# Softmax sums of two pairs of heads in one product of four 32-column blocks, one reciprocal for both, and copies across partitions inside SBUF

## The chip, the cores and the metric

One core of one Trainium2 chip. The metric is the device time of one execution, in microseconds (us). Most numbers below come from the profile of one execution of each kernel, taken on the chip; times of several executions are given as a median with the lowest and the highest.

## The reference, cut to what matters

```python
# 8 batches, 12 heads, 448 rows, 64 columns per head; fp32
q_n, k_n = rmsnorm(q, g_q), rmsnorm(k, g_k)
attn = exp(scores - max);  attn = attn / (sum(attn) + 1e-09)     # scores = q_n k_n^T / 8
x = (attn @ v), heads side by side                               # 3584 x 768
out = silu(x @ w_in) @ w_out                                     # 768 -> 2048 -> 768
```

The kernel works through 48 "pairs" of heads (8 batches x 6). It keeps everything transposed: for one pair, `xT` is 128 partitions (two heads of 64) x 448. The softmax sum of a row is therefore a sum over partitions, made by TensorE as a product with ones, and it arrives in PSUM already repeated over the 64 partitions of its head. In the first batch there are no block products of `x @ w_in` yet to fill TensorE; instead VectorE, ScalarE and GpSimd round the weights. From the second batch on, the block products ("fill") are run between the parts of the attention.

## The kernel before

The parts that the change and the argument touch. One "turn" n of the main loop, cut:

```python
for n in range(last + 2):
    scores(n, 0)                      # L400 products, L405 exponentials -> e[0], e[1]
    weigh(n - 1, 1)                   # L416
    add_up(n - 1, 2, 3); unload(n - 1)
    transpose(n + 1, "q")             # L381
    fill()                            # block products, L508 / L549 (none in the first batch)
    divide(n - 1)                     # sums L445, reciprocal L449, multiplication L451
    scores(n, 1)
    weigh(n, 0); transpose(n + 1, "k"); add_up(n, 1)      # first batch: the k transposes first
    fill()
    weights_in(n, 3); normalise(n + 3)                    # ... cut
```

```python
def add_up(n, *chunks):
    if n < z.NPAIR and 3 in chunks:       # first batch: a second partial sum
        nc.vector.tensor_tensor(out=es_two, in0=e[2], in1=e[3], op=ALU.add)
        return
    for j in chunks:
        nc.vector.tensor_tensor(out=es, in0=e[0] if j == 1 else es, in1=e[j], op=ALU.add)

def unload(n):
    nc.scalar.copy(xU, state[n]["av"])

def divide(n):
    t = ps.tile([P, S], F32, name="tr") if n >= z.NPAIR else bank(S)
    sums = [es, es_two] if n < z.NPAIR else [es]
    for i, part in enumerate(sums):
        for h in range(2):
            nc.tensor.matmul(t[ds(h * D, D), :], ones[0:R, :], part[:, h, :],
                             start=i == 0, stop=i == len(sums) - 1)
    nc.vector.reciprocal(out=r, in_=t)
    engine = nc.gpsimd if n < z.NPAIR else nc.vector
    engine.tensor_tensor(out=xT(*pairs[n]), in0=xU, in1=r, op=ALU.mult)
```

## Time and profile before

| | before |
|---|---|
| median of 4 executions | 1478.93 us (1477.04 to 1480.41) |
| span of the profiled execution | 1474.5 us |
| TensorE / VectorE / ScalarE / GpSimd busy | 1449.3 / 739.8 / 566.2 / 393.4 us |
| sum blocks (TensorE) and reciprocals (VectorE) | 48 and 48 |
| attention | up to about 850 us; then block products alone |

I read three marks, all starts of score products (L400, sixteen instructions a pair): the first of pair 1, the first of pair 7, and the second half of pair 47. "Stretch 1-7" holds turns 1 to 6; "stretch 7-47" the steady attention; what follows is the tail.

### The profile page before, as it was taken

What the parts mean: (1) busy time and instruction counts of PE and PEld (TensorE: products, weight loads), DVE (VectorE), ACT (ScalarE), POOL (GpSimd) and SP (SyncE); (2) the same over time, 40 slices, a digit from 0 to 9 for tenths busy, and PEclk for the clock granted to TensorE, in tenths of its full rate; (3) what the DMA queues carried; (4) which work ended last, traced back from release to release, by engine and by line L of the source; (5) the groups of instructions that cost most, each with busy time, mean ns of one, the idle gap of its engine ahead of it and who ended that gap; (6) DMA issues with size and microseconds to landing.
All of it is one profiled execution on the core that took longest, in us unless ns stands there. A gap on an engine that the chain in (4) does not pass through costs nothing.

```text
span 1474.5 us, 14016 instructions
## 1 busy us (share of the span) xinstructions
PE 1449.3 (98%) x5072; PEld 703.8 (48%) x5072; DVE 739.8 (50%) x928; ACT 566.2 (38%) x931; POOL 393.4 (27%) x250
## 2 busy tenths in 40 slices
PE   5999999999999999999999999999999999999998
PEld 2334444444444444444444445555555555555554
DVE  4887867676755555755554687732222222222220
ACT  5789876555555455545545444400000000000000
POOL 5864532333233333332331044410000000000000
PEclk9999999999999999999999999999999999999999
DMA  6433421221222122211211147522222222222220
GB/s 209 118 100 114 144 83 57 69 63 57 75 82 63 56 63 88 63 57 65 85 50 51 69 152 231 160 82 83 83 80 79 79 79 79 81 84 84 86 68 25
DMA packets 119188, 128.95 MB, mean 87 GB/s; under 512 B 48836, under 2 KB 101316, under 8 KB 119108
## 3 DMA queue, kind: packets, MB, share of 16 engines
q1 hardware_dynamic: 118788, 127.95, 28.2%
q8 instruction: 42, 0.69, 0.2%
q14 instruction: 38, 0.31, 0.1%
q10 hardware_dynamic: 320, 0.00, 0.0%
HBM read 87.56 MB, written 40.37 MB: 87 GB/s over the span
## 4 chain that ended last, share of the span: by engine, by line
PE 92%; DVE 5%; issue 1%; DMA 1%; ACT 0%; POOL 0%; ACTq 0%; SPq 0%; DVEq 0%; POOLq 0%
PE mm L508 35%; PE sc L508 13%; PE sc L400 9%; PE av L416 9%; PE av L508 7%; PE tr L508 7%; PE mm L549 5%; PE tr L445 3%; PE tr L386 1%; PE tr L381 1%; DVE work L449 1%; DVE rms L298 1%; DVE work L433 0%; DVE W L109 0%; DMA W<-in_moe_w_in_dram 0%
## 5 line engine op out<-in xcount | busy, mean ns | idle before, releaser
L405 ACT ACTIVATE work<-sc,rms 112x448 f32<-112x448 f32 x384 | 212.1, 636 | 183.3 <-PE sc L400 148.1
L304 POOL TENSOR_TENSOR rms<-rms,minus_half 112x16 f32<-112x16 f32 (+1 forms) x49 | 175.8, 3588 | 290.9 <-DVE rms L300 271.6
L508 PE MATMUL mm<-x,W 128*128 128x448 f32 x552 | 220.9, 541 | 0.7 <-ACT parts L515 0.6
L528 POOL TENSOR_TENSOR parts<-parts 128x448 f32<-128x448 f32 (+1 forms) x42 | 45.8, 1090 | 630.7 <-DVE parts L459 630.7
L449 DVE RECIPROCAL work<-tr 128x448 f32<-128x448 f32 x42 | 124.2, 2957 | 104.5 <-PE tr L445 104.3
L400 PE MATMUL sc<-work 64*112 64x448 f32 x768 | 170.7, 563 | 1.0 <-ACT work L382 0.6
L508 PE MATMUL mm<-sums_x,W 128*128 128x448 f32 x408 | 165.9, 542 | 0.7 <-DVE stage L459 0.4
L416 PE MATMUL av<-work,rows 112*64 112x448 f32 x768 | 165.5, 552 | 0.0
L433 DVE TENSOR_TENSOR work<-work 112x896 f32<-112x896 f32 x132 | 148.0, 1121 | 1.6
L508 PEld LDWEIGHTS mm<-x,W 128*128 128x128 f32 x552 | 101.9, 190 | 93.0 <-issue 87.9
L400 PEld LDWEIGHTS sc<-work 64*112 64x112 f32 x768 | 61.3, 173 | 103.8 <-issue 82.8
L508 PEld LDWEIGHTS mm<-sums_x,W 128*128 128x128 f32 x408 | 74.9, 190 | 68.9 <-issue 61.4
L459 DVE TENSOR_TENSOR stage<-mm,parts 128x448 f32<-128x448 f32 (+1 forms) x75 | 46.0, 614 | 118.0 <-PE mm L508 66.6
L416 PEld LDWEIGHTS av<-work,rows 112*64 112x64 f32 x768 | 46.6, 136 | 105.3 <-issue 103.8
L459 DVE TENSOR_TENSOR parts<-mm,parts 128x448 f32<-128x448 f32 (+1 forms) x50 | 30.5, 611 | 95.6 <-PE mm L508 95.2
L549 PE MATMUL mm<-x,W 128*128 128x448 f32 x192 | 75.9, 541 | 0.0
L508 PE MATMUL mm<-W,work 128*128 128x384 f32 x204 | 68.6, 486 | 0.0
L515 ACT COPY parts<-mm 128x448 f32<-128x448 f32 (+1 forms) x27 | 14.1, 523 | 141.7 <-PE mm L508 141.7
L508 PE MATMUL sc<-W,work 128*128 128x384 f32 x192 | 64.5, 486 | 0.0
L634 ACT ACTIVATE stage<-stage 128x896 f32<-128x896 f32 x56 | 50.7, 944 | 31.7 <-DVE stage L459 26.0
L405 ACT ACT_TABLE_LOAD x36 | 46.2, 1283 | 34.9 <-issue 23.8
L298 DVE TENSOR_REDUCE rms<-qn 112x8 f32<-112x512 f32 x49 | 33.3, 680 | 44.8 <-ACT qn L297 44.7
(146 smaller groups left out, 1865.0 us busy)
## 6 DMA issues: line engine op xcount, KB each, us to landing
hidden<-stage SPq DMA_DIRECT2D x56, 448.0 KB, 3.0
work<-hidden SPq DMA_DIRECT2D x7, 2048.0 KB, 9.2
x<-hidden SPq DMA_DIRECT2D x7, 2048.0 KB, 8.7
W<-in_moe_w_in_dram SPq DMA_DIRECT2D x24, 512.0 KB, 4.0
rows<-in_moe_w_out_dram SPq DMA_DIRECT2D x32, 384.0 KB, 3.6
rows<-in_q_dram SPq DMA_DIRECT2D x48, 224.0 KB, 3.5
rows<-in_k_dram SPq DMA_DIRECT2D x48, 224.0 KB, 3.3
rows<-in_v_dram SPq DMA_DIRECT2D x48, 224.0 KB, 2.5
```

The costliest lines, as they stand in the source:

```text
L298: nc.vector.tensor_reduce(out=rms[:, i], in_=t, axis=AX.X, op=ALU.add)
L304: nc.gpsimd.tensor_tensor(out=flat, in0=flat, in1=half, op=ALU.pow)
L400: nc.tensor.matmul(banks[:, h, 0:S], kT[rows, ts(j, R)], qT[n % 2][rows, :], start=True, stop=True,)
L405: nc.scalar.activation(e[j][:, h, :], banks[:, h, 0:S], AF.Exp, scale=rms[n % 4][:, 1, h, j : j + 1])
L416: nc.tensor.matmul(st["av"][ds(h * D, D), :], st["v"][:, h, j, :], e[j][:, h, :], start=(j == 0), stop=(j == J - 1),)
L433: nc.vector.tensor_tensor(out=es, in0=e[0] if j == 1 else es, in1=e[j], op=ALU.add)
L449: nc.vector.reciprocal(out=r, in_=t)
L459: nc.vector.tensor_tensor(out=out, in0=a, in1=b, op=ALU.add)
L508: nc.tensor.matmul(t, self.left(name, s), self.right(name, s), start=s == ends[0], stop=s == ends[1])
L528: nc.gpsimd.tensor_tensor(out=u2, in0=u2, in1=p5, op=ALU.add)
L549: nc.tensor.matmul(h, room.w1(c, f), xT(b, c), start=(c == 0), stop=(c == z.NW - 1))
L634: nc.scalar.activation(t, t, AF.Silu)
```

## The change

The intent: a sum needs only 32 of the 64 columns that it was given, so one block of four products (two pairs x two heads, 32 columns each) can serve two pairs, with one reciprocal of 128 partitions for both. Each reciprocal row then exists on 32 partitions and has to be copied to 64, which six small transfers inside SBUF do. Pairs whose result is needed at once (4 and 5 of the first and of the odd batches) stay single. Room for a second `es` and `r` comes from dropping `xU` (the division is now in place in `xT`) and two of the four temporaries of the block products. The first batch loses its second partial sum.

```diff
-    es_two = stage[0:R, 0 : 2 * S].rearrange("p (h s) -> p h s", h=2)
     def add_up(n, *chunks):
-        if n < z.NPAIR and 3 in chunks:
-            nc.vector.tensor_tensor(out=es_two, in0=e[2], in1=e[3], op=ALU.add)
-            return
+        t = es[n % 2]
         for j in chunks:
-            nc.vector.tensor_tensor(out=es, in0=e[0] if j == 1 else es, in1=e[j], op=ALU.add)
+            nc.vector.tensor_tensor(out=t, in0=e[0] if j == 1 else t, in1=e[j], op=ALU.add)
     def unload(n):
-        nc.scalar.copy(xU, state[n]["av"])
+        nc.scalar.copy(xT(*pairs[n]), state[n]["av"])
-    def divide(n): ...                                   # as shown above
+    def is_single(n):
+        b, hp = pairs[n]
+        return hp >= z.NPAIR - 2 and (b == 0 or b % 2 == 1)
+    def sums(members, width):
+        t = ps.tile([P, S], F32, name="tr") if members[0] >= z.NPAIR else bank(S)
+        for h in range(2):
+            for i, n in enumerate(members):
+                nc.tensor.matmul(t[ds(h * D + i * width, width), :], ones[0:R, 0:width],
+                                 es[n % 2][:, h, :], start=True, stop=True)
+        nc.vector.reciprocal(out=r[0], in_=t)
+    def divide(n, t):                                    # in place; GpSimd in the first batch
+        ...
+    def divide_by_sums(n):
+        if n > 2 and n % 2 == 1 and not is_single(n - 2):
+            for i in range(2):
+                divide(n - 3 + i, r[i])
+        if n > 0 and is_single(n - 1):
+            sums([n - 1], D)
+            divide(n - 1, r[0])
+        elif n > 0 and n % 2 == 0:
+            sums([n - 2, n - 1], D // 2)
+            own = [t.rearrange("(h i p) s -> i h p s", h=2, i=2) for t in r]
+            for i in range(2):
+                for h in range(2):
+                    nc.sync.dma_start(own[1][i, h], own[0][1, h])
+            for h in range(2):
+                nc.sync.dma_start(own[0][1, h], own[0][0, h])
     # class Seven (block products):
-            self.p1, self.u2, self.u3, self.p5 = (parts[:, ds(i * S, n)] for i in range(4))
+            self.u2, self.u3 = (parts[:, ds(i * S, n)] for i in range(2))
+            self.p1, self.p5 = done[1, 2], done[2, 1]
     # main loop:
-        if n > 0:
-            divide(n - 1)
+        divide_by_sums(n)
     # ... (allocation sizes, and an argument p1 that goes away, cut)
```

More of the change, by code (lines that the diff above doesn't have):

```diff
@@ L351, in bounded @@
     stage = mem.tile([P, 3 * 2 * S], F32, name="stage")
-    parts = mem.tile([P, 4 * S], F32, name="parts")
-    work = mem.tile([P, 15 * S + 2 * J * D], F32, name="work")
-    qT0, qT1, kT, e0, e1, e2, e3, es, xU, r = divided(
-        work, S, S, S, 2 * S, 2 * S, 2 * S, 2 * S, 2 * S, S, S
+    parts = mem.tile([P, 2 * S], F32, name="parts")
+    work = mem.tile([P, 17 * S + 2 * J * D], F32, name="work")
+    qT0, qT1, kT, e0, e1, e2, e3, es0, es1, r0, r1 = divided(
+        work, S, S, S, 2 * S, 2 * S, 2 * S, 2 * S, 2 * S, 2 * S, S, S
     )
-    qT = [qT0, qT1]
+    qT, r = [qT0, qT1], [r0, r1]
     normal, rms = normal
-    squares = work[0:R, ds(15 * S, 2 * J * D)].rearrange("p (h j d) -> p h j d", h=2, j=J)
+    squares = work[0:R, ds(17 * S, 2 * J * D)].rearrange("p (h j d) -> p h j d", h=2, j=J)
     e = [t[0:R].rearrange("p (h s) -> p h s", h=2) for t in (e0, e1, e2, e3)]
-    es = es[0:R].rearrange("p (h s) -> p h s", h=2)
+    es = [t[0:R].rearrange("p (h s) -> p h s", h=2) for t in (es0, es1)]
     def xT(b, c):
@@ L438, in divide @@
-    def divide(n):
-        t = ps.tile([P, S], F32, name="tr") if n >= z.NPAIR else bank(S)
-        sums = [es, es_two] if n < z.NPAIR else [es]
-        for i, part in enumerate(sums):
-            for h in range(2):
-                nc.tensor.matmul(
-                    t[ds(h * D, D), :], ones[0:R, :], part[:, h, :],
-                    start=i == 0, stop=i == len(sums) - 1,
-                )
-        nc.vector.reciprocal(out=r, in_=t)
-        engine = nc.gpsimd if n < z.NPAIR else nc.vector
-        engine.tensor_tensor(out=xT(*pairs[n]), in0=xU, in1=r, op=ALU.mult)
-        state[n] = None
+        nc.scalar.copy(xT(*pairs[n]), state[n]["av"])
@@ new lines, in is_single @@
+    def is_single(n):
[5 more added lines that the diff above has]
+            for i, n in enumerate(members):
+                nc.tensor.matmul(
+                    t[ds(h * D + i * width, width), :], ones[0:R, 0:width], es[n % 2][:, h, :],
+                    start=True, stop=True,
+                )
+        nc.vector.reciprocal(out=r[0], in_=t)
@@ new lines, in divide @@
+    def divide(n, t):
+        engine = nc.gpsimd if n < z.NPAIR else nc.vector
+        x = xT(*pairs[n])
+        engine.tensor_tensor(out=x, in0=x, in1=t, op=ALU.mult)
+        state[n] = None
+    def divide_by_sums(n):
[11 more added lines that the diff above has]
+                    nc.sync.dma_start(own[1][i, h], own[0][1, h])
+            for h in range(2):
+                nc.sync.dma_start(own[0][1, h], own[0][0, h])
@@ L492, in bounded, with __init__ @@
     class Seven:
-        def __init__(self, left, right, steps, n, done, p1=None):
+        def __init__(self, left, right, steps, n, done):
             self.left, self.right, self.steps, self.n, self.done = left, right, list(steps), n, done
             self.banks = {}
-            self.p1, self.u2, self.u3, self.p5 = (parts[:, ds(i * S, n)] for i in range(4))
-            if p1 is not None:
-                self.p1 = p1
+            self.u2, self.u3 = (parts[:, ds(i * S, n)] for i in range(2))
+            self.p1, self.p5 = done[1, 2], done[2, 1]
         def product(self, name, steps=None):
@@ L579, in sum_x, with part_in @@
         right_sums(*quarters(group, c), *sums_of_x(c))
-    def part_in(group, m, rows, p1=None):
+    def part_in(group, m, rows):
         chunk = 2 * m // room.CHUNK
@@ L601, in part_in @@
         done = {(i + 1, j + 1): rows[i][:, ts(j, S)] for i in range(2) for j in range(2)}
-        return Seven(lambda name, c: lefts[name](c), right, range(HW), S, done, p1)
+        return Seven(lambda name, c: lefts[name](c), right, range(HW), S, done)
     def halves_in(group, blocks, beside=lambda m: iter(()), begun=()):
@@ L752, in start @@
             rows = [staged() for _ in range(2)]
-            begun.append((rows, part_in(group, m, rows, rows[0][:, S:] if m else None)))
+            begun.append((rows, part_in(group, m, rows)))
         return begun
```

## The prediction

> **What bounds the kernel now.** I read the page's busy table and its 40 slices first, then the table of stretches, then the chain of waits in order of time, once in the attention stage with the pipeline full and once in the first batch.
>
> ```profile
> PE 1449.3 (98%) x5072; PEld 703.8 (48%) x5072; DVE 739.8 (50%) x928; ACT 566.2 (38%) x931; POOL 393.4 (27%) x250
> ...
> PE   5999999999999999999999999999999999999998
> PEld 2334444444444444444444445555555555555554
> DVE  4887867676755555755554687732222222222220
> ACT  5789876555555455545545444400000000000000
> ```
>
> TensorE looks full all the way, and VectorE and ScalarE look nearly full too, but only in the first two or three slices (37 us each). A busy TensorE proves little by itself, so the chain has to say whether its instructions really follow one another. With batches 1 to 7 running (90 to 840 us), the chain lies on TensorE almost without a break. This piece is one pair of heads and a bit; the columns are start, length, engine, line, count:
>
> ```profile
> 509.42 5.28 PE mm L508 x14
> 514.70 0.90 PE tr L445 x4
> 515.60 1.69 PE sc L400 x8
> 517.29 1.65 PE av L416 x8
> 518.95 0.53 PE tr L386 x4
> 519.48 2.27 PE mm L508 x6
> 521.75 0.04 issue
> 521.79 3.27 PE mm L508 x8
> 525.07 1.69 PE sc L400 x8
> ```
>
> L445 is the softmax sum: two products of ones with the added exponentials, one per head, in the two 64-column halves of the array. An fp32 product shows as two instructions, so x4. The block takes 0.90 us on the path. The reader should compare 514.70, where the fill products are followed by sums and then scores, with 525.07, where the scores follow the fill products directly: the scores take 1.69 us either way. So dropping a block frees its whole 0.90 us and no switching time stays behind. One pair takes 19.5 us (sums at 514.70, next at 534.22).
>
> In the first batch the chain is another:
>
> ```profile
> 35.13 0.95 DVE work L433
> 36.07 0.34 DVE W L106
> 36.41 0.02 issue
> 36.44 1.26 DVE W L109
> ...
> 39.80 1.00 DVE stage L430
> 40.81 0.04 issue
> 40.85 1.00 PE mm L445 x4
> ...
> 41.94 2.96 DVE work L449
> 44.90 0.95 DVE work L433
> ```
>
> There VectorE sets the pace: one pair every 9.77 us (35.13 to 44.90), made of adding exponentials, waiting 1.00 us for the second half of the sums, a reciprocal of 2.96 us, another add, and rounding weights. This lasts for about five pairs. After 850 us there is no attention left and the change touches only where two temporaries of the block products live.
>
> **What the skill says.** (1) "TensorE: Matmul & The Clock Gate", Part 3: products with few output columns can occupy different column groups at the same time; three 32-column tiles are given as 2.38x measured. The trace agrees for two halves: four instructions in 0.90 us, where four of the full array take 4 x 5.28/14 = 1.51 us. No trace of this kernel has four column groups; this is the main thing to find out. (2) "TensorEngine Tiling (Array Packing)", Key Properties: changing the tiling mode drains the array. The trace shows the size: 0.90 less two slots of 0.377 leaves 0.15 us. (3) "DMA: Bandwidth & Descriptors", Anatomy of one DMA: a transfer has a fixed part of about 2.0 us, mostly the receipt for the last byte, and a semaphore is waited for by the issuing sequencer, not by the DMA engines. The trace agrees in size (the table of DMA issues: KB each, then us to landing):
>
> ```profile
> rows<-in_v_dram SPq DMA_DIRECT2D x48, 224.0 KB, 2.5
> hidden<-stage SPq DMA_DIRECT2D x16, 224.0 KB, 2.0
> ```
>
> So the new copies cost latency, and they hold up the queue that issues them. (4) "Perfetto Trace Analysis", first note: matmul busy time is a bad measure of nearness to the limit. Here the chain gives a reason to trust it anyway, since instruction starts are spaced evenly.
>
> **The change, part by part.** The built program of the changed kernel, listed engine by engine, has 29 sum blocks where there were 48 (six of those double, because the first batch summed two partial tensors): 19 blocks of four 32-column products and 10 blocks of two 64-column products, the latter for pairs 4 and 5 of the first and the odd batches, whose result is needed at once.
>
> *Sum blocks on TensorE.* Outside the first batch 42 blocks become 25 (17 of four products, 8 of two). A four-product block is eight instructions; if four column groups run together that is again two slots of 0.377 plus 0.15 = 0.90 us. Removed: 17 x 0.90 = 15.3 us, all on the path by the comparison above. The weight loads of eight instructions instead of four might add something; I allow 0.1 us a block, 17 x 0.1 = 1.7 us.
>
> *Reciprocals.* 48 become 29: 19 x 2.957 = 56 us less on VectorE. Outside the first batch this is beside the path: the k transposes at L386 follow the weighting 1.65 us after its start, as do the q transposes at L381, which wait for no reciprocal. The tr bank is free in time today (in the timeline one reciprocal ends at 518.61 and the transposes start at 518.95), so nothing is gained.
>
> *First batch.* VectorE loses the reciprocal in pairs without sums and gains one add of about 0.95 us in every pair (the two partial sums were added by TensorE before). A turn without sums: 9.77 - 2.96 - 1.00 - about 0.1 of hand-over + 0.95 = 6.7 us on VectorE. A turn with sums: 9.77 + 0.95 = 10.7 us. Of the turns n = 1 to 5, sums fall in 2, 4 and 5. VectorE's own need is 3 x 10.7 + 2 x 6.7 = 45.5 us against 48.9 now, a gain of 3.4 us if the turns can lend time to each other. If they cannot, the light turns are held by ScalarE and GpSimd, busy 8.15 and 8.35 us in each 10 us there (8.0 and 8.2 per turn), and the sum is 3 x 10.7 + 2 x 8.2 = 48.5: a gain of 0.4. I take 1.8 us.
>
> *Copies inside SBUF.* 19 x 6 transfers of 57 KB on the queue that also loads q, k, v and saves hidden tiles. From the end of a reciprocal: four issues of about 0.35 us (what the v loads take), 2 us to land, two more issues, 2 us: an estimate of 6 us, so ready 1.0 + 3.0 + 6 = 10 us after the sums start. They are used by the division one pair later, 19.5 us after. In the first batch a pair takes under 10 us, but there GpSimd divides, and what it does next is for a pair two turns ahead. So I charge zero.
>
> *Divisions and temporaries.* Copying out goes straight to x and the division is in place: same counts and sizes. Two divisions now come together in every second pair; they sit before VectorE's wait for sums, of which there is plenty (104 us idle before L449). The two temporaries p1 and p5 move into the output tiles, so the copy of product 5 now waits until that tile's previous save has landed. The save starts some eight product steps (8 x 0.75 = 6 us) before the copy, and takes Silu 0.94 + landing 3.0 us: just clear. Charged zero.
>
> Sum: 15.3 - 1.7 + 1.8 = 15.4 us; 1478.5 - 15.4 = **1463 us**.
>
> **Rivals.** (a) *Four column groups don't run four at a time.* Then a four-product block costs 0.15 + 4 x 0.377 = 1.66 us, and 17 blocks give back 12.9 us: about 1475. For it: no trace here shows four; the same partitions feed all four streams. Against: two run at the full double rate. I give it one in six. (b) *The copies become the wait.* The SP queue stands still from the sums' reciprocal until the last copy is issued, about 8 us, and saves and loads behind it come late; then the copy of product 5 on ScalarE waits, exponentials behind it wait, and TensorE after them. For it: the margin of the save was only about 1 us. Against: fill work on TensorE is interrupted by 4 to 5 us of attention per half pair, which widens the margin. If a third of the pairs lose 1 us: about 1476. One in eight, small. (c) *The first batch turns over entirely*: VectorE is relieved enough that the turns follow TensorE (7.8 us without sums), about 8.5 each: gain of 6 instead of 1.8, about 1459. (d) *Something else is freed*: TensorE had nearly no idle time, so there is little to free; a gain over 2% (29.6 us) would need twice all the sum blocks that go.
>
> **Range and chances.** The steady term is counted and sure to 1 us unless (a) or (b); (c) marks the low end, with 1457 as edge; (a) and (b) the high end. Range 1457 to 1473. Faster by over 2% needs 1449: 0.02. Slower needs 1508: 0.01. Within 2%: 0.97.
>
> **What would show it right or wrong.** Right: in the chain of the changed kernel sums stand in every second pair, eight instructions in about 0.90 to 1.0 us; 29 reciprocals; VectorE busy near 740 - 56 + 6 = 690 us; between two fixed points of the steady stage (say the first and last scores of batches 2 to 7) the time is shorter by 0.90 per block dropped. (a) shows as blocks of about 1.6 us; (b) as waits of ScalarE or VectorE for a save or a copy, and pieces of the chain on the DMA queue; (c) as turns of about 8.5 us before 80 us. The prediction is wrong at its root if the steady stage shortens by under 10 or over 20 us.

## The result, and the profile after

| | before | after |
|---|---|---|
| median of 4 executions | 1478.93 us | 1469.88 us (1467.17 to 1472.12) |
| ratio to before | | 0.9939 (95% interval 0.9918 to 0.9959) |
| span of the profiled execution | 1474.5 | 1465.1 |
| start to pair 1 | 25.22 | 24.90 |
| stretch 1-7 (first batch) | 62.54 | **67.62** |
| stretch 7-47 (steady attention) | 741.00 | **726.43** |
| tail | 645.70 | 646.10 |

Ratios here and below are the mean time of one kernel's fast runs over that of the other's of the same rounds, so not quite the ratio of the medians that I quote.

The gain is 9 us where I had predicted 15. The table says where: the steady part gives 14.6 us, as worked out, and the first batch takes 5.1 back. The busy row of the changed kernel:

```profile
PE 1432.2 (98%) x5048; PEld 698.8 (48%) x5048; DVE 693.9 (47%) x915; ACT 568.7 (39%) x931; POOL 395.5 (27%) x250
```

VectorE lost 46 us (739.8 to 693.9; I had said about 690) and TensorE 17. The steady stage in the chain of the changed kernel (start, length, engine, line, count; L444 are the sums, L527 the block products):

```profile
485.75 5.28 PE mm L527 x14
491.03 0.89 PE tr L444 x8
491.92 1.69 PE sc L400 x8
...
506.01 5.28 PE mm L527 x14
511.29 1.69 PE sc L400 x8
```

Eight instructions take 0.89 us, as long as four did: four column groups run together. In the next pair the scores follow the fill directly.

The first batch, by the table of stretches: turns 1 to 5, then turn 6, the first turn of the second batch, in which pair 5's sums are made. The columns are the stretch, its length, each engine's busy time with its instructions, the granted TensorE clock, the DMA share and GB/s. First the kernel before, then the changed one:

```profile
25.22:74.97 49.75, 48.30 (x240) 17.09 (x240) 42.47 (x45) 40.36 (x78) 42.54 (x22) 1.00 0.41 112
74.97:87.76 12.79, 12.66 (x58) 4.82 (x57) 12.58 (x15) 11.25 (x21) 10.18 (x6) 1.00 0.34 92
```

```profile
24.90:73.80 48.90, 45.49 (x220) 16.30 (x221) 37.31 (x47) 40.61 (x78) 38.97 (x21) 0.97 0.49 133
73.80:92.52 18.72, 13.84 (x54) 5.16 (x53) 16.78 (x19) 11.52 (x21) 12.80 (x8) 0.82 0.18 50
```

Three things are to be seen. Turns 1 to 5 are a little shorter (49.75 to 48.90). Turn 6 is 5.9 us longer. And the granted clock, 1.00 before, is 0.97 and 0.82. VectorE's busy total over both is nearly the same, 55.05 and 54.09: two reciprocals of 2.96 us went, six adds of 1.0 to 1.1 us came. So what grew is the time in which VectorE stands, from 7.5 to 13.5 us. Here is turn 6 of the changed kernel, TensorE's timeline (start, length, then the group, idle time before it and who ended it):

```profile
77.15 0.60 PE L381 MATMUL tr<-ident,qn 112*128 112x112 f32 x4
82.63 1.76 PE L444 MATMUL mm<-work,ones 112*64 112x448 f32 x4 [4.88 <-DVE work L428]
84.32 3.06 PE L400 MATMUL sc<-work 64*112 64x448 f32 x8
```

TensorE stood 4.88 us for VectorE's adds (L428), and then the sums took 1.76 us where such a block takes 0.97 in this view of the kernel before, and the scores 3.06 where they take 1.76 in this view elsewhere. That is about half speed (the granted clock there is 0.50, see the windows under e13). What VectorE was doing is in the chain of the same time:

```profile
66.91 0.07 POOL rms L304
...
71.65 1.14 POOL x L453
...
72.82 2.96 DVE work L448
75.78 0.94 DVE work L428
...
81.48 1.10 DVE work L428
...
82.63 1.76 PE mm L444 x4
```

The reciprocal of pair 4 (72.82) waited 3.9 us for GpSimd to divide pair 2 (71.65 to 72.79), because it writes the tile that pair 2 is divided by (pair 3 is divided by the copy), and GpSimd was late because its 3.7 us power (L304) came first. So several things were suspects: the wait for the tile, the added adds, the copies, the clock.

### The profile page after: what moved, and what is told of

Read it like the earlier page. It is cut to its first block, busy times and chain, and to the rows that moved or that the text cites. A ratio compares the mean times of both kernels' runs of the same rounds, so it can differ in the third digit from the quotient of the medians.

```text
span 1465.1 us, 14059 instructions
## 1 busy us (share of the span) xinstructions
PE 1432.2 (98%) x5048; PEld 698.8 (48%) x5048; DVE 693.9 (47%) x915; ACT 568.7 (39%) x931; POOL 395.5 (27%) x250
## 4 chain that ended last, share of the span: by engine, by line
PE 91%; DVE 4%; issue 1%; POOL 1%; ACT 1%; DMA 0%; ACTq 0%; DVEq 0%; POOLq 0%
PE mm L527 36%; PE sc L527 14%; PE sc L400 9%; PE av L416 9%; PE av L527 7%; PE tr L527 7%; PE mm L568 4%; PE tr L386 2%; PE tr L444 1%; PE tr L381 1%; DVE work L428 1%; DVE work L448 1%; DVE rms L298 1%; POOL rms L304 0%; DVE sums_x L475 0%
## 5 line engine op out<-in xcount | busy, mean ns | idle before, releaser
L304 POOL TENSOR_TENSOR rms<-rms,minus_half 112x16 f32<-112x16 f32 (+1 forms) x49 | 175.9, 3590 | 292.3 <-DVE rms L300 271.4
L527 PE MATMUL mm<-x,W 128*128 128x448 f32 x552 | 220.8, 541 | 0.7 <-ACT stage L534 0.6
L527 PE MATMUL mm<-sums_x,W 128*128 128x448 f32 x408 | 165.9, 542 | 0.7 <-DVE stage L478 0.5
L428 DVE TENSOR_TENSOR work<-work 112x896 f32<-112x896 f32 x144 | 158.8, 1104 | 1.8
L527 PEld LDWEIGHTS mm<-x,W 128*128 128x128 f32 x552 | 101.8, 190 | 93.1 <-issue 88.0
L547 POOL TENSOR_TENSOR parts<-parts,stage 128x448 f32<-128x448 f32 (+1 forms) x33 | 37.2, 1128 | 314.2 <-DVE parts L478 302.7
L527 PEld LDWEIGHTS mm<-sums_x,W 128*128 128x128 f32 x408 | 74.8, 190 | 68.9 <-issue 61.5
L448 DVE RECIPROCAL work<-tr 128x448 f32<-128x448 f32 x25 | 73.9, 2956 | 49.6 <-PE tr L444 49.6
L547 POOL TENSOR_TENSOR parts<-parts,W 128x384 f32<-128x384 f32 x9 | 9.0, 995 | 307.8 <-DVE parts L478 307.8
L534 ACT COPY stage<-mm 128x448 f32<-128x448 f32 (+1 forms) x30 | 15.7, 524 | 150.0 <-PE mm L527 144.0
L478 DVE TENSOR_TENSOR stage<-mm,parts 128x448 f32<-128x448 f32 (+1 forms) x51 | 31.4, 615 | 78.5 <-PE mm L527 51.6
L527 PE MATMUL mm<-W,work 128*128 128x384 f32 x204 | 68.6, 486 | 0.0
L392 DVE TENSOR_SCALAR work<-tr,gains 128x448 f32<-128x448 f32 x36 | 24.6, 684 | 89.3 <-PE tr L386 89.3
L527 PE MATMUL sc<-W,work 128*128 128x384 f32 x192 | 64.5, 486 | 0.0
```

What stands on the lines that cost most here:

```text
L304: nc.gpsimd.tensor_tensor(out=flat, in0=flat, in1=half, op=ALU.pow)
L428: nc.vector.tensor_tensor(out=t, in0=e[0] if j == 1 else t, in1=e[j], op=ALU.add)
L448: nc.vector.reciprocal(out=r[0], in_=t)
L478: nc.vector.tensor_tensor(out=out, in0=a, in1=b, op=ALU.add)
L527: nc.tensor.matmul(t, self.left(name, s), self.right(name, s), start=s == ends[0], stop=s == ends[1])
L547: nc.gpsimd.tensor_tensor(out=u2, in0=u2, in1=p5, op=ALU.add)
```

## The experiments

Spans and stretches are those of the profiled execution. The span up to pair 1 varies from 24.9 to 27.0 us between executions without any reason that I looked into, so I judge by the stretches and not by the absolute mark that the expectations name. Each stretch is of one execution, and whether a window of half clock falls into it can move it by 1 to 2 us. A kernel marked "one run" ran once, so its state is unknown, and only its trace is used. The diffs are cut to the lines that matter.

| kernel | stretch 1-7 | stretch 7-47 | lowest clock, from pair 1 to 7 | median us | ratio to before |
|---|---|---|---|---|---|
| before | 62.54 | 741.00 | 1.0 | 1478.93 | |
| changed | 67.62 | 726.43 | 0.5 for 3.4 + 6.8 us | 1469.88 | 0.9939 |
| e1 | 67.02 | 726.41 | 1.0 | 1468.81 | 0.9937 |
| e1b | 61.94 | 726.42 | 1.0 | 1463.93 | 0.9906 |
| e2 | 66.78 | 726.39 | 0.5 for 3.4 + 6.8 us | 1467.80 | 0.9936 |
| e3 | 71.10 | 726.41 | 0.5 for 3 x 3.4 us | 1470.61 (one run) | |
| e4 | 61.43 | 726.40 | 1.0 | 1464.52 | 0.9909 |
| e4c | 61.21 | 729.73 | 0.5 for 3.4 us | 1466.47 | 0.9925 |
| e5 (wrong values) | 68.03 | 726.79 | 0.5 for 6.8 us | 1467.67 (one run) | |
| e6 (wrong values) | 70.45 | 739.26 | 0.5 for 3.4 + 6.8 us | 1484.63 (one run) | |
| e10 | 61.54 | 729.73 | 0.5 for 3.4 us | 1465.84 | 0.9920 |
| e11 | 63.89 | 726.42 | 0.5 for 6.8 us | 1464.02 (one run) | |
| e12 | **60.00** | **725.43** | 1.0 | **1460.40** | **0.9880** |
| e13 | 64.28 | 726.38 | 1.0 | 1467.21 | 0.9924 |

**e1: the first batch as before.** Each pair gets its own sums in two accumulated parts and is divided at once.

```diff
-        return hp >= z.NPAIR - 2 and (b == 0 or b % 2 == 1)
+        return b == 0 or (hp >= z.NPAIR - 2 and b % 2 == 1)
+        if n < z.NPAIR and 3 in chunks:               # in add_up
+            nc.vector.tensor_tensor(out=es_two[n % 2], in0=e[2], in1=e[3], op=ALU.add)
+            return
+                for k, part in enumerate([es, es_two]):   # innermost loop in sums
```

> The changed kernel with the first batch done as in the kernel before (own sums for every pair in two accumulated parts, no copies, GpSimd divides at once); everything later as changed. Mark: the start of the first scores of pair 7, 87.76 us in the kernel before, 92.52 in the changed one. If the whole shortfall sits in the first batch (my theory), the mark comes at 87.1 to 87.8 and the time falls by about 5 us against the changed kernel, to about 1464 us, ratio to before about 0.990. If something that lasts through the kernel costs it (the copies on the load queue, the moved temporaries), the mark comes early all the same but the stretch from pair 7 to the last scores of pair 47 is not the 726.4 us of the changed kernel, and the time stays near 1470.

A miss that was my own: 67.02, hardly better than the changed kernel. The timeline of e1 showed why (a sum block of the first batch):

```profile
52.63 0.96 PE L451 MATMUL mm<-work,ones 112*64 112x448 f32 x2
...
53.73 0.59 PE L451 MATMUL mm<-stage,ones 112*64 112x448 f32 x1
53.74 0.59 PE L451 MATMUL mm<-work,ones 112*64 112x448 f32 x1
```

I had put the loop over parts inside the loop over heads. The second head's product of the early part (`work`) stood behind the first head's product of the late part (`stage`), so only two of eight instructions were done before the late part came, and every pair got 0.74 us longer (two slots of 0.377). TensorE took its products in program order here (the `work` product at 53.74 behind the `stage` product at 53.73), so what is ready early must be put first.

**e1b: the same with the loop over parts outside**, as the kernel before has it.

> e1 repaired: there my loop put the second head's product of the early partial sum behind the late partial sum, which cost 0.74 us a pair (its mark was 93.8). Here the early part of both heads goes first, as in the kernel before. If in the first batch nothing but the pairing, the added adds and the order of products matter, the mark (first scores of pair 7) is now that of the kernel before less 0.75 us at most: 87.0 to 88.0 us, and the time about 1464 us. If the division in place or the moved temporaries cost something there, the mark stays at 89 or more.

61.94: from pair to pair exactly the times of the kernel before, less 0.6 us in the first of them. The absolute mark (88.75) was 0.75 us past my range because this execution started late (pair 1 at 26.82). The stretch 7-47 is unchanged, and the time falls to 1463.93, 6 us under the changed kernel's median. So the whole shortfall sits in the first batch, and neither the copies nor the moved temporaries cost anything later.

**e2: a reciprocal tile of its own for pairs 4 and 5**, so that nothing waits for GpSimd's reading.

```diff
-            sums([n - 1], D)
-            divide(n - 1, r[0])
+            own = r2 if n <= z.NPAIR else r[0]
+            sums([n - 1], D, own)
+            divide(n - 1, own)
```

> The changed kernel with one change: in the first batch the sums of the single pairs 4 and 5 get a reciprocal tile of their own, so VectorE needn't wait until GpSimd has read the tile of pairs 2 and 3. Theory A (this wait, 3.9 us in the trace, is the loss): the wait of the reciprocal for GpSimd is gone and the mark (first scores of pair 7) moves from 92.5 to about 88.6. Theory B (the loss is the longer row of adds on VectorE ahead of the sums): the wait only moves elsewhere and the mark stays over 91. Theory C (late copies): no change, 92.

66.78, a gain of 0.8 us, not 3.9. The wait is gone from the list, but the next instruction of VectorE, the add of two tiles in SBUF, now took 3.04 us (1.03 elsewhere) while GpSimd's three divisions ran. Theory A fails as a sufficient cause: the wait moved, as theory B had it.

**e4: as e2, with the second partial sum restored** (added by TensorE). Unfortunately with e1's loop order.

> As e2_third_r, and the first batch keeps the kernel before's two partial sums, added up by TensorE in the four 32-column blocks (accumulating), so VectorE has no added add. If A and B each cost something, the mark comes earlier than in e2, and VectorE, with two reciprocals fewer in the batch, can now gain: mark at 83 to 86 us (two reciprocals of 2.96 less than the 87.8 of before at best), time about 1461. If GpSimd's order or the copies hold the batch instead, the mark stays at 88 or later.

61.43, 5.3 us less than e2: the added adds count. It still isn't the 83 to 86 us mark that I hoped for (87.38): six reciprocals became four, but turn 6 took 15.05 us against 12.79 in the kernel before.

**e11: only the two partial sums restored** (in the right order), all else as changed.

> The changed kernel with only the two partial sums restored in the first batch (early parts first), everything else as changed: pairing, copies, one reciprocal tile. If the added adds are the loss, the stretch from pair 1's to pair 7's first scores falls from 67.6 to 61 to 63 us without the tile of their own for single pairs. If the wait for GpSimd's reading of that tile counts by itself, it stays at 65 or more.

63.89, 3.7 us less than the changed kernel. Turns 1 to 5 take 45.07 us now (48.90 in the changed kernel, 49.75 before): this is the gain that pairing was to bring. Turn 6 takes 18.82, as bad as ever, with 6.8 us at half clock. The result lies 0.9 us past my range, and the tile is the reason. Here is the reciprocal of pair 4 in the changed kernel, then in e11:

```profile
72.82 2.96 DVE L448 RECIPROCAL work<-mm 128x448 f32<-128x448 f32 x1 [3.87 <-POOL x L453]
```

```profile
69.91 2.96 DVE L455 RECIPROCAL work<-mm 128x448 f32<-128x448 f32 x1 [5.00 <-POOL x L460]
```

Without the adds the wait for GpSimd grew to 5.0 us. e4c below, which differs from e11 in this stretch by the tile of its own alone, takes 61.21: the tile is worth 2.7 us once the adds are gone (part of it half clock, 6.8 against 3.4 us), and 0.8 us while they are there (e2). Removing one cause alone leaves turn 6 long (17.82 in e2, 18.82 here); removing both gives 15.05 and 16.23 (e4, e4c).

**e3: every first-batch pair single, but the three adds in a row kept.**

> The changed kernel with every pair of the first batch single: no pairing, no copies and GpSimd's division at once there, but VectorE's three adds in a row per pair as in the changed kernel. Against e1b (two adds beside each other, summed by TensorE; 61.93 us from pair 1's to pair 7's first scores) this isolates the adds. If each added add counts in full on VectorE's chain, the stretch is 61.9 + 6 x 1.0 = 67.9 us, plus whatever half clock the longer waits of TensorE bring. If the adds are hidden and pairing is to blame, it is below 63.

71.10 us: 9.2 more than e1b, of which I had expected 6 from the adds, and half clock in three windows. So the adds cost much by themselves. But pairing isn't cleared by this: here turns 1 to 5 take 57.95 us and turn 6 takes 13.15, nearly as before (12.79), while e11, with pairing and without the adds, has turn 6 at 18.82 and is 1.95 us longer than e1b in all. The adds use up what pairing gains in turns 1 to 5; the long turn 6 comes with pairing, in part by the tile shared with GpSimd.

**e5: no copies** (values wrong).

```diff
-            ... six dma_start ...
-                divide(n - 3 + i, r[i])
+                divide(n - 3 + i, r[0])
```

> Wrong on purpose: the six copies inside SBUF are left out everywhere and both pairs are divided by the uncopied tile. Theory C (copies are the cost): the mark comes at about 88 and the steady stretch shortens too. My theory: GpSimd reaches its divisions after the copies have landed, so the mark stays within 1 us of 92.5, and the stretch from pair 7 to the last scores of pair 47 stays within 0.3 us of 726.4.

68.03 and 726.79 us: both slightly longer than with the copies. No cost of the copies shows, neither on the queue nor in the first batch. The test there isn't quite clean: in e5 both divisions read one tile, so the reciprocal of pair 4 waits for both (4.97 us instead of 3.87), and turn 4 had no half clock. The steady stretch is 0.36 off, a little past the 0.3 that I had allowed, in the wrong direction for theory C.

**e6: two column groups instead of four** (values wrong).

```diff
-                    t[ds(h * D + i * width, width), :], ones[0:R, 0:width], es[n % 2][:, h, :],
+                    t[ds(h * D, D), :], ones[0:R, :], es[n % 2][:, h, :],
```

> Wrong on purpose: the changed kernel with each block of four 32-column products made of four 64-column products instead, two on each half of the array, which overwrite one another. If the four column groups really run together in the changed kernel, each such block takes 0.15 + 4 x 0.377 = 1.66 us instead of 0.89, and the stretch from pair 7 to the last scores of pair 47 becomes 726.4 + 17 x 0.75 = 739.2 us. If they don't, it stays at 726.4.

739.26 us against the predicted 739.2, and in the chain the block takes 1.66 us:

```profile
502.23 1.66 PE tr L444 x8
503.89 1.69 PE sc L400 x8
```

So the four groups do run together in the changed kernel, and without that its steady gain would be 1.7 us instead of 14.6.

**e4c: e4 with the early parts first, and the two divisions of later batches earlier in VectorE's order.**

```diff
             unload(n - 1)
+            if n >= NPAIR:
+                divide_pairs(n)
```

> e4 with the products in that same order (early parts of both pairs and heads first), and from the second batch on the two divisions are issued earlier in VectorE's order, after the copy of av, not between the sums and their reciprocal. First: the mark, 87.4 in e4, moves to 86 to 87, because two sum blocks no longer do all their work after the late part; what stays is the add on VectorE that took 3.4 us beside three GpSimd divisions in a row. Second: the two places where the steady stretch lost 0.32 and 0.66 us (pairs 12 and 24) lose nothing, so pair 7 to the last scores of pair 47 takes 725.4 instead of 726.4. Time about 1461.

The first batch did no better than e4 (61.21): turns 1 to 5 fell from 46.38 to 44.97 us, but turn 6 rose from 15.05 to 16.23, with a window of half clock. In the steady part the losses of 0.32 and 0.66 us at pairs 12 and 24 went, as expected. But four other turns now lost 1.07 us each and the stretch grew to 729.73: the early divisions stand before VectorE's clearing of a PSUM bank, for which a block product waits. A half hit.

**e10: e4c with the divisions of the first batch on VectorE.**

> As e4c, but VectorE also does the six divisions of the first batch (pairs 0 to 3 at the end of the odd turns). Theory D: VectorE's adds with two inputs and GpSimd's multiplications hold each other up (a VectorE add took 3.43 us while three divisions ran on GpSimd, 1.03 to 1.08 otherwise; a GpSimd division took 2.13 us behind an add, 1.13 alone), so taking the divisions off GpSimd pays although VectorE gets 6 x 0.62 us more: no add over 1.2 us before the mark, mark at 84.5 to 86, time about 1460. If VectorE's load is all that counts, the mark is later than in e4c by up to 3 us.

61.54. Theory D describes real delays (the add of pair 5 takes 3.63 us in e4c and 1.00 here), but taking GpSimd out doesn't pay: VectorE then does the divisions itself on the same chain (in turns 5 and 6: 0.63 for one, 2.23 us for two). A draw, so contention for SBUF is part of the delay in turn 6 and not something that I could remove with profit.

**e13: keep TensorE busy.** The changed kernel, with products that nobody reads before the sums of turns 4 and 6.

```diff
+        count = {4: 2, 6: 6}.get(n, 0)
+        t = bank(S) if count else None
+        for _ in range(count):
+            nc.tensor.matmul(t, ident, kT, start=True, stop=True)
```

> The changed kernel with products that nobody reads put before the sum blocks of turns 4 (two) and 6 (six), each of two instructions of 0.377 us: they fit into the 1.8 and 4.9 us in which TensorE waits there for VectorE's adds. Theory E: TensorE's pauses let the granted clock fall to 0.5 (3.4 us from 59.7 and 6.8 us from 80.2 in the changed kernel, never before the end in the kernel before), and this half speed costs 1.57 us in turn 4 and 0.86 + 1.30 us in turn 6. With the products in place the clock stays at 1.00 up to 90 us, the mark (first scores of pair 7, 92.5 us) moves to 88.5 to 89.5, the time to about 1466. If the clock is a symptom and VectorE sets the time anyway, the mark stays at 91.5 or later.

Stretch 1-7 falls from 67.62 to 64.28 us by adding work. The stretches of the changed kernel from 56.26 us, then those of e13, columns as above (TensorE busy is the second number, the clock the third from the right):

```profile
56.26:59.68 3.42, 1.63 (x11) 0.57 (x12) 2.24 (x3) 0.94 (x3) 3.42 (x1) 1.00 0.40 89
59.68:63.09 3.41, 3.41 (x14) 1.31 (x12) 3.41 (x2) 2.29 (x5) 1.11 (x2) 0.50 0.00 0
76.74:80.16 3.42, 1.01 (x8) 0.39 (x4) 3.35 (x5) 3.06 (x6) 2.33 (x2) 1.00 0.20 69
80.16:83.57 3.41, 0.94 (x4) 0.30 (x4) 3.27 (x7) 1.23 (x2) 3.27 (x2) 0.50 0.00 0
83.57:86.98 3.41, 3.41 (x12) 1.08 (x8) 3.01 (x2) 0.72 (x2) 2.89 (x3) 0.50 0.13 38
```

```profile
56.26:59.68 3.42, 3.17 (x13) 1.18 (x12) 3.29 (x4) 2.64 (x6) 3.31 (x2) 1.00 1.01 224
59.68:63.09 3.41, 3.41 (x20) 1.36 (x22) 2.30 (x1) 1.43 (x3) 2.61 (x2) 1.00 0.03 8
```

In the changed kernel a window in which TensorE worked 1.63 of 3.42 us is followed by one at half clock; with filler products it worked 3.17 and the clock stayed. Theory E holds in this: the waits bring on the half clock, and filling them takes 3.3 of the 5.1 us away. The mean clock of the whole kernel says the same for every execution: 0.996 or 0.997 in the four of the changed kernel, 0.999 in the four of e13.

Two limits go with it. The waits aren't all for the added adds: e11 has none of them and 6.8 us of half clock. And where a wait falls decides. e5 has the same wait of 1.79 us in turn 4 without fillers, and kept the clock. There the wait fell across the end of a window, and the emptier of the two still had 1.86 us busy (the first row; the second is the next window, at full clock):

```profile
56.96:60.37 3.41, 1.86 (x12) 0.73 (x14) 2.22 (x3) 0.02 (x1) 3.33 (x2) 1.00 0.19 54
60.37:63.79 3.42, 3.42 (x22) 1.23 (x20) 3.42 (x3) 3.29 (x7) 0.84 (x1) 1.00 0.37 88
```

e13 also starts pair 1 2.05 us later than the changed kernel, so its fillers at turn 4 may not have been what kept the clock there; of its 3.3 us, 1.3 lie in turns 1 to 5 and 2.1 in turn 6. The page "TensorE: Matmul & The Clock Gate", Part 1, of the Trainium skill states such a throttle with a window of 3413 ns; the trace agrees with the length (3.41 and 6.83 us), but it happened after a pause of 1.8 us and not of a whole idle window. The medians differ by 2.7 us, but they are of different rounds and the two intervals of the ratio overlap (0.9907 to 0.9940 here), so the stretch and the clock are the evidence. The absolute mark (91.22) is again past my range, with pair 1 at 26.95 in this execution.

**e12: what seemed best together**: two partial sums, early parts first, an own tile for pairs 4 and 5, the divisions early only in turns where a single sum follows, two filler products in turn 6.

```diff
+    def goes_early(n):
+        return z.NPAIR <= n < 5 * z.NPAIR and n % 2 == 1 and is_single(n - 1)
```

(In the code the bound 5 x 6 lets this be turns 11 and 23 alone, and not 35 and 47, which the expectation names too.)

> Meant as the best version: two partial sums in the first batch, early parts first, an own tile for single pairs, the two divisions moved early only in the turns where a single sum follows (11, 23, 35, 47), and two unread products before the sums of turn 6 to keep the clock up. Start of pair 1 to first scores of pair 7: 61.2 us in e4c, here 59.9 to 60.5 (the 1.3 us of half clock gone); pair 7 to the last scores of pair 47: 725.4 us (the changed kernel's 726.4 less 0.98). Time 1460 to 1462, ratio to before 0.988 to 0.990. If moving the divisions early hurts also there, the second stretch is 726 or more.

60.00 and 725.43 us, both as expected, the clock at 1.00 throughout: 1460.40 us (1459.20 to 1461.92), 0.9880 of before (0.9864 to 0.9897). It is faster than the kernel before by 1.2% and than the changed one by about 0.6%. What is left in it is turn 6, 14.62 us: an add of VectorE beside three GpSimd divisions, in the chain

```profile
67.00 2.96 DVE stage L457
69.95 3.66 DVE work L433
```

instead of the usual 0.95. "SBUF — State Buffer", Who interferes with whom, says that a VectorE instruction with two SBUF inputs contends with a GpSimd instruction that reads SBUF, and that the later one blocks fully; this row agrees: GpSimd's third division ends at 72.67, and the add at 73.61, one add of 0.94 us later.

## Why the prediction was right or wrong, by its own steps

The time lay in the range, but the middle was off by 7 us (1463 against 1469.9), and the result fell into the part of the range that I had kept for rivals (a) and (b), neither of which happened. That the range held was luck in so far. The mechanism of the steady stage was right. The terms of its sum:

- *Sum blocks, 15.3 us*: right. 17 blocks went, each gave 0.90 us, and the stretch 7-47 gained 14.57 and not 15.3 mainly because two turns lost 0.98 elsewhere. (That the 0.15 us left beside the slots is the draining of the array was a reading; e6 shows the same rest, 1.66 less four slots, and no run tells its cause.) *Allowance for eight weight loads, 1.7 us*: not needed, the block takes 0.89.
- *First batch, +1.8 us*: the step that failed; it measured -5.1. Its parts: (1) For turns 1 to 5 I had 45.5 to 48.5 us on VectorE against 48.9; measured 48.90 against 49.75, of which about 1.6 us in turn 4 are half clock that no step had. So the estimate of the turns was usable. (2) I stopped counting at turn 5. The single sums of pair 5 are made in turn 6, and there 12.79 became 18.72 us. The chain shows the greater part of why: "there GpSimd divides, and what it does next is for a pair two turns ahead. So I charge zero" left out that pair 4's reciprocal writes the tile by which GpSimd still has to divide pair 2. It waited 3.9 us for that, 5.0 in e11. (3) I took VectorE's relief for granted from 19 fewer reciprocals; in this stage it is two (5.9 us) against six added adds (about 6.5), so there was none. e11 shows what pairing gives there without the adds: turns 1 to 5 in 45.07, which turn 6 then takes back. (4) I took TensorE's idle time as free where it isn't the limit. It cost a second time, as half clock: up to 3.3 us by e13.
- *Divisions in twos, charged zero*: wrong by 0.98 us. "They sit before VectorE's wait for sums, of which there is plenty" is true on average, but in turns 11 and 23 a single sum follows in the same turn and the fill leaves no such wait; the reciprocal started 1 us late and the k transposes waited for it (0.32 and 0.66 us). e12 removed this and nothing else in that stretch.
- *Copies, charged zero*: right (e5). The issue took 0.58 us and not the 0.35 of the v loads, and the landing 1.9, and in turn 4 of the changed kernel the last issue ended 4.5 us after the reciprocal, so the copies were there after about 6 us, as estimated.
- *Temporaries, charged zero*: right, as far as e1b shows: pair by pair the times of the kernel before, and tails of 645.7 to 646.5 in all kernels.
- Rivals: (a), groups not together, is refuted by the 0.89 us and by e6 (its time, by the sum's own terms, was 1476 and not 1475). (b), copies as the wait, is refuted for the steady stage by e5. (c), the first batch following TensorE, did not come; in e11 the five turns got to 9.0 us each. No rival had the first batch get worse. Yet the profile before held the warning: VectorE at eight tenths in those slices, and on the chain.

What stays open: how the 1.7 us of the loss that remain without half clock (64.28 in e13 against 62.54) divide among the adds, the wait for the tile and contention with GpSimd. These don't add up singly: restoring the partial sums gave 3.7 us, the tile 0.8, and both 6.2 to 6.4 (e4, e4c).

## What to carry to other kernels

A change that pays in the stage that holds most of the time can cost in a short stage with another limit; work out each stage to its end, including the first place where a later stage waits for the backlog. Before giving an adding-up back to an engine, look whether that engine sets the pace there: six adds took what two reciprocals gave. Before one tile serves two users, look at who reads it last: a reciprocal waited 3.9 us for a slow reader. And a wait of the matrix engine of 1.8 us brought its clock down for the next 3.4 us in one kernel and not in another, so in a tight stage it is worth looking at the granted clock by stretches, and even filler products can pay.

## What the Trainium skill lacked or had wrong

- "TensorE: Matmul & The Clock Gate", Part 1, and its rule against idle gaps over about 3.4 us: here half clock followed windows that were not idle, with TensorE busy 1.63, 1.01 and (e4c) 1.49 of 3.42 us; pauses of 1.8 and 1.9 us were enough. With each run's windows laid end to end from its first clock record, the fullest window that half clock followed had 1.65 us busy (e6, from 58.44 us), and up to the last products the emptiest after which full clock stayed had 1.86 (e5, above): in these runs the limit lies between, near half a window. Busy time alone isn't the whole of it, since e6 kept full clock after 1.49 us at its very last products (from 1474.97 us).
- The same page, Part 3, has no number for four column groups with 112 rows and fp32: eight instructions took 0.89 us, as long as four in two groups (0.90), and the same number in two groups 1.66 us.
- "DMA: Bandwidth & Descriptors": an issue time only as a count of sequencer cycles, and none measured for small copies inside SBUF. Here 0.51 to 1.04 us each (median 0.58 for the first four, 0.51 for the last two), with 1.9 us to landing for 56 KB. The section that the prediction cites for the fixed 2.0 us is written for GpSimd's queue; these copies went through SP's.
- "SBUF — State Buffer", Who interferes with whom: agrees; the size for fp32 is added here: an add of 112 x 896 took 3.66 us instead of 0.95 to 1.03 behind three multiplications of 128 x 448 on GpSimd.
